# Two layers of linear attention and squared-relu feed-forward: one more pair of tiles by the seven block products in each layer

## The chip, the cores and the metric

The kernel runs on one core of one Trainium2 chip. The metric is the device time of one execution in microseconds (us), the median of several runs. The engines are named as in the profile: PE multiplies matrices (PEld is its loading of weights), ACT applies functions and copies, DVE and POOL do elementwise arithmetic, SP issues most DMA transfers. Each engine carries out its own instructions in the order in which the program names them, and waits where an operand is not there yet.

## The reference

There are 2048 tokens of width D = 640. Two layers, with the same weights, each an attention block and a feed-forward block:

```python
x = x + A(layernorm(x))      # attention, 32 heads of 20
x = x + B(layernorm(x))      # feed-forward, hidden width 1728
x = x + A(layernorm(x))
x = x + B(layernorm(x))

A(x): q, k, v = x @ wqkv, by heads; phi(t) = where(t > 0, t + 1, exp(t)) + 1e-6
      kv = sum over tokens of phi(k) v;  z = sum over tokens of phi(k)
      o  = (phi(q) @ kv) / (phi(q) . z + 1e-6);  returns o @ wo
B(x): h = relu(x @ w1 + b1)**2;  returns h @ w2 + b2
```

All of it is float32. The result is the last x.

## The kernel before

**Tiles and groups.** The tokens are 16 tiles of 128, in 4 groups of 4 tiles (`NT`, `TG`, `NG`). A float32 product is made as three passes of a reduced form: each operand is split into a high part (a rounded copy) and a low part (the rest), and PE adds high x low, low x high and high x high (`mm3`, whose matmuls have line 508).

**Attention, folded.** Since kv is one small matrix for each head, kv and wo are multiplied into one matrix M of 640 x 640 before the feed-forward part of a layer. The attention output of a tile is then phi(q), divided by its denominator, times M. M lies in five row blocks of 128, `M[0]` to `M[4]`, each with its high and low part.

**Feed-forward.** For each group there is FC1 (x @ w1) in 14 chunks c = 0 to 13 of the hidden width (`fc1`, L1234, 15 matmuls of 128x512 for each, 10 for the last), each followed on ACT by relu and square (`act`, L1245 and L1246), and FC2 (h @ w2) in 28 steps (`fc2_step`, L1317). FC2 is made by a scheme that forms a 2 x 2 block product from seven block products instead of eight. Its operands are formed on ACT (`u_hi`, L1289), DVE (`u_lo`, L1298; `s_op`, L1263).

**The attention output inside FC1.** During FC1 of group g the attention output of the next group's four tiles is made. There are two ways:

- `single(g, i)`: one tile. 30 matmuls (L508) at PE after chunk `OUTS[i]` = 4, 7, 10 or 13, into PSUM banks 6 and 7; its operand is the whole tile, split high and low at once (`p_split`, L1345 on ACT, L1347 on DVE).
- `pair(g, j)`: two tiles together, by seven block products of M's 2 x 2 blocks (each 256 x 320) and one piece for the last 128 rows of M ("rest"): 54 matmuls (L1528). They stand at four chunks, `c0 + 4` to `c0 + 7`, where `c0` is `PAIR_AT[j]`, 1 or 6: products 1, 5 and a rest piece `d` at the first, 6 and 2 at the second, 7 and 3 at the third, 4 at the last. The operands are seven blocks of 128 x 256 (`hi`, L1474 on ACT; `lo`, L1478 on DVE), of which four are sums made first on DVE (`s_op` inside `pair`, L1471), and two rest pieces (`rest_hi`, `rest_lo`, L1492). The results are added to x on DVE (L1539).

Ahead of either way each tile is prepared. phi(q) is loaded (`b_load_pq`, SP), its denominator made on DVE (`b_den`: a product L744 and a sum L747), it is divided and turned in 32 x 32 blocks on DVE (`b_blocks`: L753, L754, L756, L465), and ACT moves the blocks to their places (`blocks_move`, L474: four instructions of 32 x 160 for each of four block rows). x is loaded (`b_load_x`). After the output: norm statistics on DVE and POOL (L397, L399, L401, L402), the norm (L407) and its store to DRAM (L435), and the addition of b2 on POOL (`f_bias`, L1214). Then the normed tile is loaded again, turned and split for the next FC1 (`x_in`).

**M's block sums.** A pair needs four blocks (m4, m5, m6, m7) that are sums or differences of blocks of M. `mix_M(g)` makes them in the FC1 of group `MIX_G[layer]`, 1 in layer 0 and 0 in layer 1: `whole` (DVE, L1598), `mix` (POOL, L1609), `high` (ACT, L1618), `low` (DVE, L1622), and `store` (SP, L1626 to L1628), which keeps them in DRAM. `place` (SP, L1631) loads the kept m5 into the upper halves of `M[0]` and `M[1]`. Before, it stands in FC2 behind that FC1, at steps 4 and 8. The others are loaded as units when a pair needs them.

**What sets the order.** Nothing is planned by costs. Every piece of side work is put in a list of events by hand: `at(g, n, f)` puts `f` behind chunk n, or (n >= 14) behind FC2 step n − 14; `on` does the same for a tile's work, where a negative chunk falls into FC2 of the group before, or, for group 0, at chunk 0. Behind each chunk the loop issues in this order: the chunk's matmuls, the next unit's load, relu and square, the products that stand at this chunk, and then the chunk's events in the order in which they were entered: `mix_M` first, then FC2's operands (`ffn_events`), then singles, then pairs. Before, a group with g > `MIX_G` has two pairs, others (but the last group) have four singles.

**Weights.** The units of w1, of w2's seven block products and of m4, m6, m7 are loaded on SP into a ring of six buffers (`RING`, `load_ring`, L371) in the order of their use, which `uses_of` lists. A load is issued once a buffer was used. In group 0, `load_stay` (L381) also loads seven resident FC2 units, one behind each of the chunks 3 to 9.

Of the kernel before, what the change touches and what calls it, by code (L numbers as in the profile page):

```python
# [19 lines left out]
NF = 14  # L20
FL = F - 13 * P
TG = 4
# [4 lines left out]
NG = NT // TG  # L27
# [33 lines left out]
MIX_G = (1, 0)  # L61
# [11 lines left out]
def kernel(  # L73
# [141 lines left out]
    def uses_of(layer):  # L215
        uses = []
        for g in range(NG):
            for c in range(NF):
                uses.append((g, "w1", c))
                if MIX_G[layer] < g < NG - 1:  # L220
                    for j, c0 in enumerate(PAIR_AT):
                        if c0 + 5 <= c <= c0 + 7:
                            uses.append((g, ("m6", "m7", "m4")[c - c0 - 5], j))
            uses += [(g, m, k) for m in ORDER for k in range(1, PAIRS)]
        return uses

# [241 lines left out]
    def blocks_move(yz, js):  # L468
        if len(yz) == 1:
            yz.append(ftile("z"))  # L470
        yv, zv = (a.rearrange("p (c j q) -> p c j q", c=DC, q=B32) for a in yz)
        for j in js:
            for i in range(P // B32):
                nc.scalar.activation(  # L474
                    zv[j * B32 : (j + 1) * B32, :, i, :], yv[i * B32 : (i + 1) * B32, :, j, :], AF.Copy
                )
# [90 lines left out]
    for layer in range(N_LAYERS):  # L567
# [156 lines left out]
        def b_load_pq(t):  # L724
            if t < NT:
                pq[t] = ftile("pqt")
                nc.sync.dma_start(pq[t], pqd[t])
# [9 lines left out]
        def b_load_x(t):  # L737
            xr[t] = x1_at(t)
            nc.sync.dma_start(xr[t], src[t])
# [28 lines left out]
        def b_den(t):  # L768
            b_step(t, 2)

        def b_blocks(t):
            b_step(t, 3)
# [69 lines left out]
        for t in range(NT):  # L842
# [54 lines left out]
            g = list(range(DC)) if t > 0 else []  # L897
# [463 lines left out]
        def at(g, n, f):  # L1361
            events.setdefault((g, n), []).append(f)
# [59 lines left out]
        def after(g):  # L1422
            def on(n, f):
                if n < 0 and g > 0:
                    at(g - 1, NF + N_STEPS + 2 * n, f)
                elif n >= NF:
                    at(g, NF + int(2 * (n - NF)), f)
                else:
                    at(g, max(n, 0), f)

            return on
# [134 lines left out]

        def pairs(g):
            on = after(g)
            both = [pair(g, j) for j in range(2)]
            for p in both:  # L1570
                next(p)
            for i, moves in enumerate(MOVES_AT):
                t = TG * (g + 1) + i
                on(PQ_AT[i], lambda t=t: b_load_pq(t))
                on(DEN_AT[i], lambda t=t: b_den(t))
                on(TURN_AT[i], lambda t=t: b_blocks(t))
                for n, q in moves:
                    on(n, lambda t=t, q=q: blocks_move(yzp[t], (q,)))
                on(PAIR_AT[i // 2] + 1, lambda t=t: b_load_x(t))
                x_in(g, i)  # L1580
            for p in both:
                next(p, None)

        def mix_M(g):
            first = (g * N_STEPS + 2) % SLOTS * 4 * HT + 2 * HT
            v = arena.rearrange("p s j k n -> p (s j k n)")[:, first : first + 4 * D]
            h = [R[:, i, 1].rearrange("p c n -> p (c n)")[:, HT + D * j : HT + D * (j + 1)] for i in range(2) for j in range(2)]
            a, b, q = (h[0], h[3]), (h[1], h[0]), (h[2], h[1])
            if g == 0:
                x1 = x1_odd["tile"]  # L1590
                b, q = (h[1], x1[:, 2]), (h[2], x1[:, 3])
            oq = v[:, : 2 * D].rearrange("p (j m n) -> p j m n", j=2, m=2)
            o6, o4 = (v[:, D * i : D * (i + 1)].rearrange("p (j n) -> p j n", j=2) for i in (2, 3))
            lo, hi = slice(0, HD), slice(HD, D)

            def whole(p):
                for out, m in ((a[p], p), (b[p], 2 + p)):
                    nc.vector.tensor_tensor(  # L1598
                        out=out, in0=M[m][:, 0].bitcast(F32), in1=M[m][:, 1].bitcast(F32), op=ALU.add
                    )  # L1600

            def mix(p):
                for out, x, y, op in (
                    (q[p][:, lo], a[p][:, hi], a[p][:, lo], ALU.subtract),
                    (q[p][:, hi], b[p][:, hi], a[p][:, hi], ALU.subtract),
                    (a[p][:, hi], q[p][:, hi], a[p][:, lo], ALU.add),
                    (b[p][:, lo], b[p][:, lo], a[p][:, hi], ALU.subtract),
                ):
                    nc.gpsimd.tensor_tensor(out=out, in0=x, in1=y, op=op)  # L1609

            def parts(p):
                return (
                    (oq, q[p].rearrange("p (m n) -> p m n", m=2)), (o6, a[p][:, hi]), (o4, b[p][:, lo]),
                )

            def high(p):
                for u, x in parts(p):
                    nc.scalar.activation(u[:, 0], x, AF.Copy)  # L1618

            def low(p):  # L1620
                for u, x in parts(p):
                    nc.vector.tensor_tensor(out=u[:, 1], in0=x, in1=u[:, 0].bitcast(F32), op=ALU.subtract)  # L1622

            def store(p):
                for i, m in enumerate(("m5", "m7")):
                    nc.sync.dma_start(kept[m, 0][:, :, p], oq[:, :, i].bitcast(F32))  # L1626
                nc.sync.dma_start(kept["m6", 0][:, :, p], o6.bitcast(F32))
                nc.sync.dma_start(kept["m4", 0][:, :, p], o4.bitcast(F32))  # L1628

            def place(p):  # L1630
                nc.sync.dma_start(M[p][:, :, HD:].bitcast(F32), kept["m5", 0][:, :, p])  # L1631

            for c, f, p in (
                (0, whole, 0), (0, mix, 0), (2, high, 0), (3, low, 0), (3, store, 0), (3, whole, 1),
                (3, mix, 1), (5, high, 1), (6, low, 1), (6, store, 1),
            ) if g else (
                (1, whole, 0), (1, mix, 0), (2, whole, 1), (2, mix, 1), (3, high, 0), (4, low, 0), (4, store, 0),
                (5, high, 1), (6, low, 1), (6, store, 1),
            ):
                at(g, c, lambda f=f, p=p: f(p))  # L1640
            for p in range(2):
                at(g, NF + 4 + 4 * p, lambda p=p: place(p))

        def ffn_events(g):
            for k in range(PAIRS):
# [69 lines left out]
        for g in range(NG):  # L1715
            ffn_events(g)
        for g in range(NG - 1):
            if g > MIX_G[layer]:
                pairs(g)
                continue  # L1720
            for i in range(TG):
                single(g, i)
        side_last()
        if layer == 0:
            prep_last()
# [1 line left out]
        for g in range(NG):  # L1727
# [9 lines left out]
            last = N_STEPS - PAIRS  # L1737
# [46 lines left out]
```

## Time and profile before

| | us |
|---|---|
| median of 3 runs | 1313.88 (1313.72 to 1313.97) |
| the profiled execution | 1314.4 |
| its span | 1312.7 |
| PE busy | 1305.7 (99%) |
| DVE busy | 920.8 (70%) |
| ACT busy | 745.9 (57%) |
| POOL busy | 237.4 (18%) |
| layer 0, FC1 of group 1 (the edited one), start to end | 361.97 to 426.12 |
| layer 1, FC1 of group 0 (the edited one), start to end | 904.55 to 968.70 |

Matmuls are busy time of PE, weight loads that of PEld, and the two overlap. A row of a timeline has the start in us, the length in us, the engine, the line of the kernel, the operation, its output and inputs by the program's names with their shapes, and a count where several are taken together. Brackets at the end give the idle time of the engine just ahead of it and what ended that. The granted clock of PE is 1.00 of full speed over the whole run.

### The profile page before, as it was taken

How to read it: one execution, taken by the hardware profiler on the slowest of the kernel's cores; microseconds unless marked ns; L12 is line 12 of the kernel's file. 1: busy time of each engine (PE TensorE's matmuls, PEld its weight loads, DVE VectorE, ACT ScalarE, POOL GpSimd, SP SyncE). 2: the span in 40 equal slices, each digit the busy share in tenths (PEclk: the TensorE clock that was granted, in tenths of full speed). 3: DMA queues.
4: the chain of work that ended last, by engine and by line, in shares of the span. 5: the costliest groups of instructions: out<-in, count | busy, mean ns of one | idle time of the engine just before them, and what ended most of it. 6: DMA issues, size and time to landing. Idle time of an engine off the chain costs nothing.

```text
span 1312.7 us, 21122 instructions
## 1 busy us (share of the span) xinstructions
PE 1305.7 (99%) x7441; PEld 1188.5 (91%) x7441; DVE 920.8 (70%) x1685; ACT 745.9 (57%) x1648; POOL 237.4 (18%) x305
## 2 busy tenths in 40 slices
PE   9999999999999999999999999999999999999998
PEld 8888888989988988998988889989899899889888
DVE  7888957757965976843856677677779479579145
ACT  5888967785486476334423232387755834944242
POOL 2334310054032102101012222002330030021000
PEclk9999999999999999999999999999999999999999
DMA  6898985699996996998954456544889779879756
GB/s 195 246 277 268 307 244 168 253 349 386 324 329 213 286 366 229 286 369 297 348 179 126 126 136 173 148 166 176 322 282 373 270 253 324 302 252 314 287 188 220
DMA packets 143071, 339.94 MB, mean 259 GB/s; under 512 B 17318, under 2 KB 67622, under 8 KB 142326
## 3 DMA queue, kind: packets, MB, share of 16 engines
q1 hardware_dynamic: 135734, 316.31, 70.2%
q0 software_dynamic: 7232, 22.29, 6.6%
q8 instruction: 59, 0.97, 0.3%
q14 instruction: 46, 0.38, 0.1%
HBM read 255.92 MB, written 70.78 MB: 249 GB/s over the span
## 4 chain that ended last, share of the span: by engine, by line
PE 93%; DVE 2%; ACT 2%; DMA 1%; issue 0%; SPq 0%; POOL 0%; ACTq 0%; DVEq 0%; POOLq 0%
PE PS L508 30%; PE PS L1234 28%; PE PS L1317 26%; PE PS L1528 4%; PE PS L535 3%; ACT z L494 1%; PE PS L1069 1%; PE PS L1082 1%; DMA st<-in_B_w_dram 1%; PE PS L865 0%; PE PS L656 0%; DMA kept<-uprep 0%; DVE xT L524 0%; DVE uprep L331 0%; DVE r L618 0%
## 5 line engine op out<-in xcount | busy, mean ns | idle before, releaser
L1234 PE MATMUL PS<-xTb,u 128*128 128x512 f32 x1640 | 378.9, 390 | 0.0
L1234 PEld LDWEIGHTS PS<-xTb,u 128*128 128x128 f32 x1640 | 306.4, 188 | 61.7
L508 PE MATMUL PS<-kq,xT 128*128 128x320 f32 (+2 forms) x1575 | 284.4, 335 | 1.4 <-DVE xT L524 1.4
L508 PEld LDWEIGHTS PS<-kq,xT 128*128 128x128 f32 x1575 | 250.4, 188 | 29.1 <-DVE xT L524 2.0
L1317 PE MATMUL PS<-u,arena 128*128 128x320 f32 x1644 | 250.6, 310 | 0.0
L1317 PEld LDWEIGHTS PS<-u,arena 128*128 128x128 f32 x1644 | 243.4, 188 | 0.4
L474 ACT ACTIVATE z<-y 32x160 f32<-32x160 f32 x512 | 171.1, 334 | 40.4 <-DVE y L465 34.5
L1298 DVE TENSOR_TENSOR arena<-R,arena 128x512 fp32r<-128x512 f32 (+1 forms) x200 | 135.2, 682 | 83.0 <-ACT arena L1289 82.6
L1289 ACT ACTIVATE arena<-R 128x512 fp32r<-128x512 f32 (+1 forms) x200 | 116.2, 592 | 132.0 <-PE PS L1317 100.3
L1245 ACT ACTIVATE R<-PS,b1sb 128x512 f32<-128x512 f32 x104 | 71.4, 686 | 116.8 <-PE PS L1234 116.1
L508 PE MATMUL PS<-kh,xh 128*128 128x512 f32 x480 | 124.4, 393 | 0.0
L401 POOL TENSOR_SCALAR rs<-mv 128x1 f32<-128x1 f32 x64 | 32.5, 507 | 475.8 <-DVE mv L399 475.1
L1317 PE MATMUL PS<-uw,arena 128*128 128x320 f32 x660 | 106.1, 309 | 0.0
L508 PEld LDWEIGHTS PS<-kh,xh 128*128 128x128 f32 x480 | 87.3, 188 | 15.2 <-DVE xT L524 0.2
L1317 PEld LDWEIGHTS PS<-uw,arena 128*128 128x128 f32 x660 | 99.2, 188 | 0.3 <-DVE x L1331 0.2
L1263 DVE TENSOR_TENSOR R<-R 128x512 f32<-128x512 f32 (+1 forms) x128 | 88.5, 694 | 14.8 <-ACT R L1246 14.8
L494 ACT ACTIVATE z<-y 32x160 f32<-32x160 f32 x272 | 90.9, 334 | 3.3
L610 ACT ACTIVATE r<-PS 128x512 f32<-128x512 f32 (+1 forms) x64 | 27.6, 433 | 96.6 <-PE PS L508 95.5
L617 DVE TENSOR_SCALAR r<-r 128x512 f32<-128x512 f32 (+1 forms) x64 | 21.3, 332 | 69.7 <-ACT r L610 69.6
L1246 ACT ACTIVATE R<-R 128x512 f32<-128x512 f32 x104 | 65.8, 633 | 3.3
L1331 DVE TENSOR_TENSOR x<-PS,x 128x320 f32<-128x320 f32 x112 | 53.0, 484 | 19.2 <-PE PS L1317 18.4
L1539 DVE TENSOR_TENSOR x<-PS,x 128x320 f32<-128x320 f32 x48 | 23.2, 489 | 45.5 <-PE PS L1528 44.9
(155 smaller groups left out, 1548.4 us busy)
## 6 DMA issues: line engine op xcount, KB each, us to landing
u<-kept SPq DMA_DIRECT2D x113, 640.0 KB, 5.7
u<-kept_w SPq DMA_DIRECT2D x104, 640.0 KB, 5.6
u<-kept SPq DMA_DIRECT2D x56, 320.0 KB, 6.4
kept<-uprep SPq DMA_DIRECT2D x49, 320.0 KB, 5.3
z<-xb SPq DMA_DIRECT2D x160, 80.0 KB, 4.9
u<-kept_m SPq DMA_DIRECT2D x18, 640.0 KB, 4.9
pqt<-pq SPq DMA_DIRECT2D x32, 320.0 KB, 6.4
acc<-r POOLq DMA_DIRECT2D x28, 320.0 KB, 5.3
```

The source lines that it names most:

```text
L474: nc.scalar.activation(zv[j * B32 : (j + 1) * B32, :, i, :], yv[i * B32 : (i + 1) * B32, :, j, :], AF.Copy)
L494: nc.scalar.activation(zv[j * B32 : (j + 1) * B32, :, i, :], yv[i * B32 : (i + 1) * B32, j], AF.Copy)
L508: nc.tensor.matmul(ps, a, b, start=first and i == 0, stop=last and i == 2)
L1234: nc.tensor.matmul(ps, a[:, d, :], bb[:, d, :], start=(d, i) == order[0], stop=(d, i) == order[-1],)
L1245: nc.scalar.activation(r, v, AF.Relu, bias=b1sb[:, c : c + 1])
L1246: nc.scalar.activation(r, r, AF.Square)
L1263: nc.vector.tensor_tensor(out=quad(*out, k), in0=quad(*x, k), in1=quad(*y, k), op=op)
L1289: nc.scalar.activation(u[:, 0], v, AF.Copy)
L1298: nc.vector.tensor_tensor(out=u[:, 1], in0=v, in1=u[:, 0].bitcast(F32), op=ALU.subtract)
L1317: nc.tensor.matmul(ps, x, y, start=opens and k == 0 and p == 0 and e == 0, stop=k == PAIRS - 1 and p == b - a - 1 and e == len(seq) - 1, s ...
L1331: nc.vector.tensor_tensor(out=v, in0=ps, in1=v, op=ALU.add)
L1528: nc.tensor.matmul(ps, x, y, start=m in (1, 5, 2, "d") and i == 0 and e == 0, stop=i == len(todo) - 1 and e == 2, skip_group_check=True,)
```

## The change

In the FC1 of group `MIX_G[layer]`, the tiles 0 and 1 of the next group stay singles, and tiles 2 and 3 become a pair (j = 1, products at chunks 10, 11, 12 and 13). So each layer has one pair more and two singles fewer. Since a pair's preparation stands at other chunks than a single's, the steps of tiles 2 and 3 move: their denominators are at chunks 1 and 3 (were 4 and 7), their block turns at 2 and 4 (were 5 and 8), ACT's moves at 3, 4, 5, 5 for tile 2 and 6, 6, 7, 7 for tile 3 (were 5, 5, 6, 6 and 8, 8, 9, 9), the loads of phi(q) in the FC2 before, or at chunk 0 where there is none (were at chunks 2 and 5), the loads of x both at chunk 7 (were 7 and 10), and the norms at chunk 13 and behind it (were 12 and behind 13). `place` moves from FC2 to chunk 7 of that FC1. The ring gets the units m6, m7 and m4 there: m6 just ahead of the last w1 unit and m7 and m4 just behind it.

```diff
@@ uses_of
-                if MIX_G[layer] < g < NG - 1:
+                if MIX_G[layer] <= g < NG - 1:
                     for j, c0 in enumerate(PAIR_AT):
-                        if c0 + 5 <= c <= c0 + 7:
+                        if (g > MIX_G[layer] or j) and c0 + 5 <= c <= c0 + 7:
                             uses.append((g, ("m6", "m7", "m4")[c - c0 - 5], j))
+            if g == MIX_G[layer]:
+                ms = [v for v in uses if v[0] == g and v[1] != "w1"]
+                last = (g, "w1", NF - 1)
+                uses = [v for v in uses if v not in ms + [last]] + ms[:1] + [last] + ms[1:]
             uses += [(g, m, k) for m in ORDER for k in range(1, PAIRS)]
@@ pairs
-            both = [pair(g, j) for j in range(2)]
+            js = range(2) if g > MIX_G[layer] else (1,)
+            both = [pair(g, j) for j in js]
             for p in both:
                 next(p)
             for i, moves in enumerate(MOVES_AT):
+                if i // 2 not in js:
+                    continue
@@ mix_M
             for p in range(2):
-                at(g, NF + 4 + 4 * p, lambda p=p: place(p))
+                at(g, 7, lambda p=p: place(p))
@@ the list of events
         for g in range(NG - 1):
-            if g > MIX_G[layer]:
+            for i in range(TG if g < MIX_G[layer] else 2 if g == MIX_G[layer] else 0):
+                single(g, i)
+            if g >= MIX_G[layer]:
                 pairs(g)
-                continue
-            for i in range(TG):
-                single(g, i)
```

## The prediction

> **What bounds the kernel now.** I read first the page's busy times, then the busy time by stretches, the chain that ended last by pieces inside the two FC1s that the change edits, and last each engine's timeline there.
>
> ```profile
> span 1312.7 us, 21122 instructions
> PE 1305.7 (99%) x7441; PEld 1188.5 (91%) x7441; DVE 920.8 (70%) x1685; ACT 745.9 (57%) x1648; POOL 237.4 (18%) x305
> ```
>
> PE is busy for 1305.7 of 1312.7 us: what takes matmuls away shortens the kernel, and what makes PE wait lengthens it by the whole wait. The next columns are busy time of PE, PEld, DVE, ACT, POOL, then PE clock, DMA share and GB/s. The first row is FC1 of layer 0 with the block sums (its group 1), the second that of layer 1 (group 0), the third an FC1 of layer 1 with two pairs, the fourth six microseconds inside the second:
>
> ```profile
> 361.97:426.12 64.15, 64.15 (x327) 56.08 (x327) 35.75 (x65) 46.71 (x106) 19.05 (x21) 1.00 0.77 271
> 904.55:968.70 64.15, 64.15 (x328) 56.08 (x327) 46.03 (x72) 46.77 (x107) 26.95 (x26) 1.00 0.84 306
> 1010.94:1073.41 62.47, 62.47 (x316) 54.30 (x315) 37.71 (x78) 42.96 (x104) 7.65 (x10) 1.00 0.75 266
> 934.00:940.00 6.00, 6.00 (x38) 5.65 (x37) 4.82 (x8) 3.99 (x12) 1.38 (x2) 1.00 1.03 393
> ```
>
> In all of them PE never waits; ACT is busy for 69 to 73 per cent of the FC1s, and the DMA queues are full in the fourth (share 1.03). That share is an average; what counts is whether ACT is in time where PE takes over its work, so the chain by pieces (start, length, what) and ACT's timeline follow, in layer 1's edited FC1:
>
> ```profile
> 925.98 10.22 PE PS L1234 x45
> 936.20 4.39 PE PS L508 x30
> 940.60 10.22 PE PS L1234 x45
> 950.82 4.39 PE PS L508 x30
> ...
> 1056.37 2.20 PE PS L1528 x15
> 1061.99 2.19 PE PS L1528 x15
> 1067.61 2.19 PE PS L1528 x15
> 1072.10 1.31 PE PS L1528 x9
> ```
>
> ```profile
> 922.15 2.77 ACT L474 ACTIVATE z<-y 32x160 f32<-32x160 f32 x8 [2.89 <-DVE y L465]
> 924.94 0.69 ACT L1245 ACTIVATE R<-PS,b1sb 128x512 f32<-128x512 f32 x1
> 926.20 1.44 ACT L1618 ACTIVATE arena<-R 128x640 fp32r<-128x640 f32 x3
> 931.70 0.72 ACT L1345 ACTIVATE pTs<-z 128x640 fp32r<-128x640 f32 x1
> 939.72 0.69 ACT L1245 ACTIVATE R<-PS,b1sb 128x512 f32<-128x512 f32 x1
> 940.98 0.62 ACT L1289 ACTIVATE arena<-R 128x512 fp32r<-128x512 f32 x1
> ```
>
> ACT is late here already. The x45 from 925.98 are chunks 5, 6 and 7, 10.22 / 3 = 3.41 each, so chunk 6 ended at 936.20 − 3.41 = 932.8; its relu (L1245) runs at 939.72, 6.9 us behind. Before, nobody waits for that: a single needs one split tile per 10 to 14 us.
>
> **The change part by part.** *Matmuls.* Two singles leave, 30 matmuls of 4.39 us each: 8.78. A pair comes, 2.20 + 2.19 + 2.19 + 1.31 = 7.89. Saved 0.89 us per layer, 1.78 in all. The third stretch above agrees: two pairs in place of four singles, 64.15 − 62.47 = 1.68, 0.84 each. It is a gain only as long as PE still never waits.
>
> *When the pair wants its operands.* Products 1, 5 and the rest piece come behind chunk 10, at 950.82 in layer 1, the rest behind chunks 11, 12, 13. A product of six matmuls costs 6/15 of 2.19, 0.88, so product 5 is wanted at 951.7 and the rest piece at 952.6.
>
> *Layer 1, ACT's queue.* Tiles 6 and 7 now have their block turns at chunks 2 and 4, and ACT's moves at 3, 4, 5, 5 and 6, 6, 7, 7, where they were two and three chunks later. Everything below is in the order in which ACT gets it. The start: tile 5's moves began at 922.15 when DVE had turned it; in the new order DVE does the product and sum for tile 6's denominator first:
>
> ```profile
> 921.27 0.84 DVE L465 STREAM_TRANSPOSE y<-pqt 128x640 f32<-128x640 f32 x1
> 943.62 0.81 DVE L744 TENSOR_TENSOR y<-pqt,zbc 128x640 f32<-128x640 f32 x1
> 944.47 0.82 DVE L747 TENSOR_REDUCE den<-y 128x32 f32<-128x640 f32 x1
> 952.23 0.68 DVE L1263 TENSOR_TENSOR R<-R 128x512 f32<-128x512 f32 x1
> 952.83 0.61 DVE L407 TENSOR_SCALAR xn<-x,mv,rs 128x640 f32<-128x640 f32 x1
> ```
>
> that is 0.81 + 0.82, so 922.15 + 1.65 = 923.8. From there ACT has no gap that I can find, because every move's turn is done ahead of it: 12 block-row moves (tiles 5, 6, 7; a row is 4 instructions, 2.77 / 2 = 1.385) 16.6; relu and square of chunks 3 to 8, 926.20 − 924.94 = 1.26 each, 7.6; the block sums' two high halves, 1.47 with the hand-over, 2.9; tile 5's split 0.63; three FC2 splits (L1289) at 0.6, 1.8; and the pair's first two high halves. Those are in the rows of the pairs in later groups:
>
> ```profile
> L1474 ACT ACTIVATE pTs<-z x42: 400/402/420, 480.6 to 1168.7; 128x256 fp32r<-128x256 f32 x42
> L1478 DVE TENSOR_TENSOR pTs<-z,pTs x42: 381/418/3823, 481.1 to 1170.1; 128x256 fp32r<-128x256 f32 x42
> L1492 DVE TENSOR_TENSOR pTs<-z,pTs x12: 283/284/286, 485.0 to 1158.4; 128x128 fp32r<-128x128 f32 x12
> ```
>
> 0.8 for two. Sum 30.3, so product 5's high half is there at 954.1. The FC2 split just before it, done at 953.7, releases DVE for four instructions in order: L1298 0.69, L1263 0.68, the norm of tile 5 0.61, and then product 5's low half 0.42: 956.1. PE wants it at 951.7. Product 1 is in the same queue: four items of ACT (the FC2 split 0.6, relu and square 1.26, two moves 2.77, and its own high half 0.4) nearer its front, its low half behind these two and tile 5's adds on DVE,
>
> ```profile
> 946.91 0.88 DVE L1412 TENSOR_TENSOR x<-PS,x 128x320 f32<-128x320 f32 x2
> 947.71 0.88 DVE L397 BATCH_NORM_STATS2 bn<-x 128x6 f32<-128x320 f32 x2
> ```
>
> some 2.6 us behind 948.8, at 951.8, so PE waits about 1.0 before product 1 and 3.4 before product 5. **Together 4.4 us.**
>
> *Layer 1, the rest piece.* Its low halves (two L1492, 0.28) are next on DVE, after 956.4. Then the biases of tiles 3 and 5 sit together on POOL, since tile 3's was at chunk 10 already and tile 5's waits for tile 5's norm. What that does to a DVE instruction with two inputs:
>
> ```profile
> 940.03 3.11 POOL L1214 TENSOR_TENSOR x<-x,b2bc 128x640 f32<-128x640 f32 x2
> 941.63 2.07 DVE L1298 TENSOR_TENSOR arena<-R,arena 128x512 fp32r<-128x512 f32 x1 [2.71 <-ACT arena L1289]
> 946.30 0.69 DVE L1298 TENSOR_TENSOR arena<-R,arena 128x512 fp32r<-128x512 f32 x1 [1.02 <-ACT arena L1289]
> ```
>
> 2.07 us where the same one takes 0.69 when POOL is idle: it was held until POOL's bias ended. One held instruction costs at least 0 (rest halves first) and at most two of 1.4, 2.8; I take 2.0, nearer the upper end because both biases are released by the norm that stands ahead of the low half. The Trainium skill, "SBUF — State Buffer", section "Who interferes with whom", says that a vector instruction with two SBUF inputs and a GpSimd instruction that reads SBUF exclude each other for the whole instruction; this trace agrees (2.07 against 0.69), and by it the sum below stays, while mere sharing would at most double the two instructions, 0.6 in place of 2.0, and the sum would be 3.5.
>
> *Layer 0.* Same queue, with more slack: ACT had gaps,
>
> ```profile
> 374.85 2.77 ACT L474 ACTIVATE z<-y 32x160 f32<-32x160 f32 x8
> 386.85 0.69 ACT L1245 ACTIVATE R<-PS,b1sb 128x512 f32<-128x512 f32 x1 [3.08 <-PE PS L1234]
> ...
> 408.24 4.40 PE PS L508 x30
> ```
>
> the moves start at 374.85 + 1.65, and 0.8 more because tile 10's load of 320 KB now stands ahead of tile 9's in the queue (0.33 MB at the 393 GB/s of the fourth stretch): 377.3. One block-sum half less lies behind that point (30.3 − 1.5): product 5's high half 406.1, low half 408.2. PE wants it at 408.24 + 0.88 = 409.1. Margin 0.9; the rest piece behind a bias of POOL may miss by some tenths: **0 to 0.4, taken 0.3.**
>
> *The moved load of the block sums into the matrix, and the extra units.* The kept m5 is loaded back at chunk 7 now, where before it was in FC2. In layer 1 the store before it is the last of these:
>
> ```profile
> 939.64 1.03 SPq L1628 DMA_DIRECT2D kept_m<-arena  x1
> DMA to landing us min/median/max: 8.4/8.4/8.4
> ...
> DMA to landing us min/median/max: 6.4/6.9/7.4
> ```
>
> (the second landing row is that of the load back, L1631). SP takes its queue in order: the stores come at about 941 (their high halves leave ACT at 939.4, 14.7 us of the 30.3 before product 5's), then m6's load, which waits for m6's store, then the two loads back. With the tiles' loads now all ahead of chunk 1 the queue is emptier, so I take some 5 us for the store and not 8.4, and 6.4 to 7.4 for the loads back: 952 to 954. That is after 951.7 and before 956.1: covered by the low half, and next in line if ACT turns out earlier. In layer 0, where PE wants them at 409.1, the stores are past well before: ACT's queue had the gap of 3.08 us there, and the same sum ends at 402 to 405. Behind them on SP wait the x tiles, resident units and chunk 13's weights, the x tiles with about 2 us to spare, chunk 13's weights, used after 960, with more than 5; taken 0. The two loads that leave FC2 were hidden by PE: 0. Eight adds for four, and the norms one chunk later, have the following FC2 as cover: 0. More loads of units: 3 of 640 KB in each FC1, 0.77 and 0.84 of DMA share leave room: 0.
>
> *Sum.* −1.78 + 4.4 + 2.0 + 0.3 = +4.9. The profiled run took 1314.4 us, 0.5 over the median of the runs, 1313.88; the change is of one kind on both, so 1313.88 + 4.9 = **1318.8 us**, slower by 0.37 per cent. About 0.2 per cent, 2.6 us, is what a measurement of this kernel can tell from no change.
>
> **The rivals.** *A, nothing waits.* ACT's gaps are wider than I count and the halves come before 951.7: 1313.88 − 1.78 = **1312.1**. For it: the pairs in other groups run without a wait. Against: there no block sums, singles' splits and biases share the chunks, and here it needs 4.4 us less than the 30.3 that I count. This is the rival on the other side. It decides from the point where product 5's low half lands by 951.7.
>
> *B, a smaller wait.* ACT is 1 to 3 us earlier (fewer items behind a late turn) or the biases do not hold the rest piece: waits of 1 to 4 us, 1313 to **1316.4**. If ACT is early, the load of m5, 952 to 954, is what ends last: 0.3 to 2.3 us.
>
> *C, as forecast.* 4.4 and 2.0 stand to within 2 us: 1316.6 to 1320.8.
>
> *D, late loads.* The load of m5 lands after the low half, because the queue is full: a DMA share of 1.03 stood when the 8.4 us landing began. If the store takes these 8.4 us again from 941, and the loads back, issued at 949.5, do so too, they land at 958 to 959, 2 to 3 us after 956.1: up to **1321.8**.
>
> *E, PE's clock.* A gap could make TensorE run slower for a while. The longest gap of PE in the trace is
>
> ```profile
> 172.13 3.05 PE L508 MATMUL PS<-kq,xT 128*128 128x320 f32 x19 [1.18 <-DVE xT L524]
> ```
>
> 1.18 us, and the clock is 1.00 in every stretch shown, so rows give no drop up to there. If after the 3.4 us before product 5 the clock were half for as long as the gap was, 1.7 us of its work would be left over: **1320.5**. The Trainium skill, "TensorE: Matmul & The Clock Gate", section "What's actually happening", gives half rate after at least one idle window of about 3.4 us; no run here shows it yet.
>
> **How the numbers follow.** C 0.54, A 0.14, B 0.22, D 0.05, E 0.05. The predicted time is that of C. The range runs from A's 1312.0 to 1321.0; C's own is 1316.6 to 1320.8. Faster by over 0.2 per cent needs 1311.25, 0.9 us more than A gives: 0.03, out of A's. The rest of A and B lie within 0.2 per cent, up to 1316.5: 0.33. C, D and E: 0.64.
>
> **What would show it.** In the changed profile: PE's waits in layer 1's edited FC1, by name: product 1 and 5 for L1478, the rest piece for L1492, and layer 0's without one; the FC1's length, 64.15 − 0.9 + 6.4 = 69.7, against 63.3 to 63.7 in layer 0; ACT without an idle row from 923.8 to 954; POOL's two L1214 at about 956. If PE waits for uM's load instead, the m5 load was the bound; if nobody waits, ACT's queue was mis-summed.

## The result, and the profile after

| | before | after |
|---|---|---|
| median of the runs, us | 1314.47 (6 runs) | 1319.84 (6 runs) |
| the profiled execution, us | 1314.4 | 1319.76 |
| FC1 with the block sums, layer 0 | 64.15 | 63.31 |
| FC1 with the block sums, layer 1 | 64.15 | 68.72 |

The changed kernel is slower: the ratio is 1.0037, with a 95% interval of 1.0026 to 1.0047. 1318.8 us had been forecast, a ratio of 1.0037 to the median known then.

In the changed kernel's profile line numbers are 4 to 7 higher than before (behind L1420 one more in the kernels A to D below). The head of the page and the first line of the chain that ended last, and behind them that line of the kernel before:

```profile
span 1318.0 us, 21177 instructions
PE 1305.7 (99%) x7429; PEld 1186.3 (90%) x7429; DVE 931.1 (71%) x1715; ACT 749.2 (57%) x1662; POOL 239.1 (18%) x305
PE 89%; ACT 4%; DVE 3%; DMA 2%; issue 1%; SPq 1%; POOL 0%; ACTq 0%; DVEq 0%; POOLq 0%
...
PE 93%; DVE 2%; ACT 2%; DMA 1%; issue 0%; SPq 0%; POOL 0%; ACTq 0%; DVEq 0%; POOLq 0%
```

The share of ACT and DVE in the chain has grown. The stretches of the two edited FC1s show where (length, then busy time of PE, PEld, DVE, ACT, POOL, then the clock, DMA share, GB/s):

```profile
361.49:424.80 63.31, 63.31 (x322) 55.18 (x321) 38.80 (x75) 48.10 (x113) 17.56 (x19) 1.00 0.81 294
905.08:973.80 68.72, 64.38 (x322) 55.18 (x321) 48.98 (x84) 48.39 (x114) 24.54 (x24) 1.00 0.82 302
```

Layer 0 saves 0.84 us and PE waits nowhere in it. In layer 1, 68.72 − (64.15 − 0.84) = 5.4 us are lost: 68.72 − 64.38 = 4.3 as idle time of PE, and 64.38 − 63.31 = 1.1 in PE's rows around it, which count as busy. PE's timeline of the changed kernel names what it waited for (idle time ahead of a row, and what ended it, in brackets):

```profile
664.40 13.68 PE L512 MATMUL PS<-kq,xT 128*128 128x512 f32 x66 [1.40 <-DMA kq<-kept_kq]
...
936.95 0.41 PE L512 MATMUL PS<-uM,pTs 128*128 128x320 f32 x1 [0.22 <-ACT pTs L1349]
939.06 4.52 PE L512 MATMUL PS<-uM,pTs 128*128 128x320 f32 x29 [1.70 <-DVE pTs L1351]
953.64 1.04 PE L1532 MATMUL PS<-uM,pTs 128*128 128x320 f32 x6
955.63 0.41 PE L1532 MATMUL PS<-uM,pTs 128*128 128x320 f32 x1 [0.95 <-ACT pTs L1478]
957.52 1.44 PE L1532 MATMUL PS<-uM,pTs 128*128 128x320 f32 x8 [1.47 <-DVE pTs L1482]
```

Two places of layer 1 stand out: the single product of tile 5 waits for its split, and product 5 of the pair waits for its high and then its low half. The row at 664.40 is at the start of layer 1, where layer 1's projection weights kq are loaded; it is dealt with below. The spans of the two profiled executions differ by 5.3 us, and −0.84 in layer 0's edited FC1, 4.57 in layer 1's and 1.40 at that row make 5.1 of it; the stretches ahead of these places, between them and behind them change by no more than 0.5 us each. The queue behind the waits, on ACT and DVE of the changed kernel, and the two places where POOL's additions of b2 meet DVE:

```profile
925.20 2.78 ACT L478 ACTIVATE z<-y 32x160 f32<-32x160 f32 x8 [5.39 <-DVE y L469]
955.18 0.40 ACT L1478 ACTIVATE pTs<-z 128x256 fp32r<-128x256 f32 x1
```

```profile
936.93 2.07 DVE L1351 TENSOR_TENSOR pTs<-z,pTs 128x640 fp32r<-128x640 f32 x1 [1.07 <-ACT pTs L1349]
957.04 0.42 DVE L1482 TENSOR_TENSOR pTs<-z,pTs 128x256 fp32r<-128x256 f32 x1
957.71 0.49 DVE L1496 TENSOR_TENSOR pTs<-z,pTs 128x128 fp32r<-128x128 f32 x2
```

```profile
936.79 1.54 POOL L1218 TENSOR_TENSOR x<-x,b2bc 128x640 f32<-128x640 f32 x1
957.49 0.64 POOL L439 DMA_DIRECT2D xb<-xn  x1 [3.61 <-DVE pTs L1482]
958.16 5.14 POOL L1218 TENSOR_TENSOR x<-x,b2bc 128x640 f32<-128x640 f32 x2
```

ACT starts tile 5's moves at 925.20, 20.1 us behind FC1's start, and ends product 5's high half at 955.58, 30.4 us later, without an idle row between. DVE ends the low half at 957.46 and PE goes on at 957.52. The split of tile 5 (L1351) started while POOL's first addition ran and took 2.07 us in place of 0.77. The rest halves (L1496) came before POOL's next two additions, ahead of which POOL first issued the store of tile 5's norm (L439), and were not held; there it was POOL that took 5.14 us for two in place of 3.1.

### The profile page after: what moved, and what is told of

It is laid out like the page before. It is cut to its first block, busy times and chain, and to the rows that moved or that the text cites. A ratio compares the mean times of both kernels' runs of the same rounds, so it can differ in the third digit from the quotient of the medians.

```text
span 1318.0 us, 21177 instructions
## 1 busy us (share of the span) xinstructions
PE 1305.7 (99%) x7429; PEld 1186.3 (90%) x7429; DVE 931.1 (71%) x1715; ACT 749.2 (57%) x1662; POOL 239.1 (18%) x305
## 4 chain that ended last, share of the span: by engine, by line
PE 89%; ACT 4%; DVE 3%; DMA 2%; issue 1%; SPq 1%; POOL 0%; ACTq 0%; DVEq 0%; POOLq 0%
PE PS L512 27%; PE PS L1238 26%; PE PS L1321 25%; PE PS L1532 5%; PE PS L539 3%; ACT z L478 1%; PE PS L1073 1%; PE PS L1086 1%; DMA kq<-kept_kq 1%; ACT z L498 1%; DMA st<-in_B_w_dram 1%; DMA pqt<-pq 0%; PE PS L869 0%; PE PS L660 0%; DVE uprep L335 0%
## 5 line engine op out<-in xcount | busy, mean ns | idle before, releaser
L1543 DVE TENSOR_TENSOR x<-PS,x 128x320 f32<-128x320 f32 x64 | 30.9, 489 | 56.4 <-PE PS L1532 55.6
L1335 DVE TENSOR_TENSOR x<-PS,x 128x320 f32<-128x320 f32 x112 | 53.2, 486 | 18.6 <-PE PS L1321 17.9
```

What stands on the lines that cost most here:

```text
L1335: nc.vector.tensor_tensor(out=v, in0=ps, in1=v, op=ALU.add)
```

## The experiments

The theory: in layer 1 ACT's queue, begun late behind DVE and without a gap, sets when product 5's operand is there; layer 0 has slack. The rivals: a cost that the extra units and loads spread over the kernel (the sum of the stretches above leaves it next to nothing); POOL's hold of DVE; the load of m5. The table has, for each kernel, the length of layer 1's edited FC1, the time from its start to the start of the next FC1, both from its one profiled execution, and the ratio of its runs to those of the kernel before with the 95% interval. "c" marks profiles in which PE's clock fell in that stretch, which costs 1.7 us of PE's work (below).

| kernel | FC1 | FC1 + FC2 | ratio to before |
|---|---|---|---|
| before | 64.15 | 106.39 | |
| changed | 68.72 | 111.13 | 1.0037 (1.0026 to 1.0047) |
| pair in layer 0 alone | 64.15 | 106.76 | 0.9997 (0.9988 to 1.0006) |
| pair in layer 1 alone | 68.62 c | 111.03 | 1.0038 (1.0024 to 1.0051) |
| splits later | 70.5 c | 113.46 | 1.0040 (1.0026 to 1.0054) |
| additions of b2 into FC2 | 70.2 c | 117.78 | 1.0075 (1.0063 to 1.0088) |
| denominator later | 68.63 c | 111.01 | 1.0033 (1.0021 to 1.0046) |
| splits later, additions spread | 65.8 | 112.63 | 1.0042 (1.0030 to 1.0055) |
| these two, and denominator later | 67.6 c | 113.78 | 1.0049 (1.0036 to 1.0062) |
| these three, and m5 by POOL | 64.8 | 111.02 | 1.0037 (1.0023 to 1.0051) |
| A: splits and denominator later, additions early | 67.9 c | 110.87 | 1.0032 (1.0019 to 1.0044) |
| B: A, m5 first, units from chunk 7 | 64.26 | 108.77 | 1.0018 (1.0009 to 1.0027) |
| C: A, m5 first | 65.69 | 108.69 | 1.0011 (1.0002 to 1.0020) |
| D: A, m5 first, units from chunk 5 | 64.26 | 109.39 | 1.0017 (1.0008 to 1.0026) |

### One layer at a time

The conditions on `MIX_G` in the change were made to hold in one layer alone:

```diff
-                if MIX_G[layer] <= g < NG - 1:
+                if MIX_G[layer] + (layer == 1) <= g < NG - 1:
```

for layer 0 alone, with `layer == 0` for layer 1 alone, and so at the other places of the change. Expected:

> The changed kernel with the extra pair in layer 0 alone; layer 1 is as before. Theory (ACT's queue in layer 1 is late, layer 0 has slack): FC1 of group 1 in layer 0 takes 63.3 us, 0.84 less than before, PE waits nowhere in it, and the whole kernel is 0.8 us faster than before, within 0.2 per cent. Rival (the extra units and the moved loads cost something elsewhere, such as the 1.4 us that PE waited for kq at the start of layer 1): 0.5 to 1 us slower than before.

> The changed kernel with the extra pair in layer 1 alone; layer 0 is as before. Theory: all of the loss is here: FC1 of group 0 in layer 1 takes 68.7 us (64.15 - 0.84 + 5.4 of waits), the kernel is 4.6 us slower than before. Rival (a part of the loss comes from layer 0's edit, by way of kq): about 3 us slower.

Layer 0 alone: the stretch of its edited FC1, and PE's wait for kq from the table of waits (us in all, times, longest):

```profile
362.06:425.37 63.31, 63.31 (x322) 55.17 (x321) 38.77 (x75) 47.88 (x113) 17.55 (x19) 1.00 0.83 294
```

```profile
PE PS L512 <- DMA kq<-kept_kq: 0.4, 1, 0.4
```

The 0.84 us are saved, with no wait; over the whole kernel they can't be told from no change, and the rival's 0.5 us slower can't be excluded by the time alone (the interval ends at 0.8 us). Layer 1 alone costs as much as the whole change. So the loss is layer 1's. As for kq: the twelve profiled kernels with the pair in layer 0 run the same instructions up to there, and their waits for kq are 1.40, 0.38, 0.56, 1.19 and 1.29 us in five and none in seven; it differs from execution to execution, and nothing in layer 1's edits decides it. Whether the pair in layer 0 makes it likelier stays open: the two profiles without that pair (before, and layer 1 alone) show none.

Layer 1 alone showed something else. PE's timeline at tile 5's product, and the clock (eighth column) around it:

```profile
937.69 6.06 PE L512 MATMUL PS<-uM,pTs 128*128 128x320 f32 x29 [1.72 <-DVE pTs L1351]
956.08 1.44 PE L1532 MATMUL PS<-uM,pTs 128*128 128x320 f32 x8 [1.08 <-DVE pTs L1482]
```

```profile
936.00:938.00 2.00, 0.31 (x2) 0.31 (x3) 1.64 (x1) 1.92 (x5) 0.96 (x1) 0.99 1.03 396
938.00:940.00 2.00, 2.00 (x9) 2.00 (x8) 1.06 (x2) 1.96 (x5) 0.00 (x0) 0.50 1.02 422
940.00:942.00 2.00, 2.00 (x11) 2.00 (x11) 1.09 (x3) 1.94 (x6) 0.49 (x1) 0.65 1.05 420
```

29 matmuls took 6.06 us, where the changed kernel's took 4.52. The clock fell to half after a wait of 1.9 us, and 2 x 0.50 + 2 x 0.35 = 1.7 us of work were lost by it. Here that cost nothing more: product 5 was late anyway, and its wait shrank from 2.4 to 1.1 us. The Trainium skill, "TensorE: Matmul & The Clock Gate", section "What's actually happening", gives half rate after at least one idle window of about 3.4 us and calls the window free-running; the half rate agrees with this row, the drop after only 1.9 us of idle time does not agree with a full idle window.

### What stands ahead of product 5

FC2's splits in this FC1 later:

```diff
             for k in range(PAIRS):
-                at(g, 6 + k, lambda k=k: u_hi(g, k))
-                at(g, 7 + k, lambda k=k: u_lo(g, k))
+                n = (9, 9, 10, 11)[k] if layer == 1 and g == 0 else 6 + k
+                at(g, n, lambda k=k: u_hi(g, k))
+                at(g, n + 1, lambda k=k: u_lo(g, k))
```

(and the sums behind them at 11, 12, 13, the fifth split at 12).

> The changed kernel with FC2's first splits and sums in layer 1's group 0 three chunks later (ACT's splits at 9, 9, 10, 11 and 12, were 6 to 9 and 11). ACT has three splits of 0.6 us less ahead of product 5's high half, and DVE one split and one sum (0.69 + 0.68) less between it and the low half. Theory (ACT's queue): low half some 3 us earlier, at 954.5; the wait of 3.1 us before product 5 falls to 0.5, that of 2.3 us before tile 5's product stays; FC1 66.0 us; the kernel 2.6 us faster than the changed one. Rival (the load of m5 into the matrix, issued at 947.6 and 948.5 and landed 6.8 us later, ends next): 955.4 in place of 954.5, 1 us of the wait stays and is named for the DMA; the kernel 1.7 us faster than the changed one.

It did not get faster, which neither the theory nor the rival had. The rows of ACT, DVE, POOL and PE at product 5:

```profile
951.70 0.40 ACT L1478 ACTIVATE pTs<-z 128x256 fp32r<-128x256 f32 x1
```

```profile
952.13 3.63 DVE L1482 TENSOR_TENSOR pTs<-z,pTs 128x256 fp32r<-128x256 f32 x1 [0.74 <-ACT pTs L1478]
```

```profile
952.43 3.04 POOL L1218 TENSOR_TENSOR x<-x,b2bc 128x640 f32<-128x640 f32 x2
```

```profile
955.81 1.96 PE L1532 MATMUL PS<-uM,pTs 128*128 128x320 f32 x8 [2.36 <-DVE pTs L1482]
```

The high half came 48.9 us behind FC1's start (903.24), 1.6 us earlier than in the changed kernel (955.58 − 905.08 = 50.5); three splits of 0.6 had been expected. But the low half now fell on POOL's two additions and was held for 3.2 us, so it ended where it had ended before. After the wait the clock fell to 0.62 and 0.52 for 2 us each, 1.7 us more. A hold by POOL is what the prediction had put on the rest piece; here it hit product 5's low half.

The additions of b2 of tiles 1 to 3 were then taken out of FC1, all to FC2's start:

```diff
-            at(0, 4 + 2 * t, lambda t=t: f_bias(t))
+            at(0, NF if layer == 1 and t else 4 + 2 * t, lambda t=t: f_bias(t))
```

> The changed kernel with the additions of b2 to tiles 1, 2, 3 on POOL in layer 1's group 0 moved out of FC1 into the start of FC2. Theory (one queue on ACT sets when product 5 can start, and the wait before tile 5's product only takes a part of it ahead): tile 5's low half takes 0.8 us in place of 2.07, PE's wait before tile 5's product falls by 1.3 us, the wait before product 5 grows by the same, FC1 stays at 68.7 within 0.4. Rival (the held instruction of DVE is a loss by itself, and the waits add up): FC1 67.4 us, the kernel 1.3 us faster than the changed one.

The wait before tile 5's product fell from 1.9 to 0.6 us (0.17 and 0.45), as both expected. The pair's waits, which still ended with product 5's halves, grew from 2.4 to 3.4 us (0.48, 1.44 and 1.47), and without the 1.7 us of the clock FC1 is 68.5 us. That is the theory's 68.7 and not the rival's 67.4: ACT's queue sets the end of the pair, and the held split only took a part of the wait ahead. But FC2 paid. POOL, DVE and PE in its first steps:

```profile
978.63 5.33 POOL L1218 TENSOR_TENSOR x<-x,b2bc 128x640 f32<-128x640 f32 x3
```

```profile
984.43 3.75 DVE L1267 TENSOR_TENSOR R<-R 128x512 f32<-128x512 f32 x1
```

```profile
988.57 1.00 PE L1321 MATMUL PS<-u,arena 128*128 128x320 f32 x5 [1.99 <-DVE arena L1302]
```

DVE, which forms FC2's operands, was held there (3.75 us for a sum that takes 0.68 a few rows later), PE waited for it, the clock fell a second time behind that wait (0.67 and 0.50 over 4 us, another 1.7 us), and FC1 and FC2 together are 117.8 us. Neither theory had FC2 in it.

The start of the queue:

```diff
-                on(DEN_AT[i], lambda t=t: b_den(t))
+                on(DEN_AT[i] + (g == 0 and i == 2), lambda t=t: b_den(t))
```

> The changed kernel with the denominator of tile 6 one chunk later in layer 1's group 0 (chunk 2, behind tile 5's turn, in place of chunk 1 ahead of it). Theory (a queue on ACT without a gap, begun late by the 1.65 us of DVE that now stand ahead of tile 5's turn): ACT's moves begin 1.65 us earlier relative to FC1's start, 18.5 us behind it in place of 20.1, and everything behind them too; FC1 67.1 us in place of 68.7 where PE's clock stays whole. Rival (another wait comes next at once, DVE held by POOL, or the load of m5): FC1 stays above 68.

```profile
924.54 2.77 ACT L478 ACTIVATE z<-y 32x160 f32<-32x160 f32 x8 [3.82 <-DVE y L469]
```

```profile
955.14 0.39 PE L1532 MATMUL PS<-uM,pTs 128*128 128x320 f32 x1 [1.66 <-ACT pTs L1491]
956.80 2.11 PE L1532 MATMUL PS<-uM,pTs 128*128 128x320 f32 x8 [1.28 <-DVE pTs L1482]
```

FC1 starts at 906.02 here, so the moves start at 18.5, 1.6 us earlier, as expected. Tile 5's product does not wait at all. Product 5 does, for 2.9 us, and the clock fell behind it, so FC1 is 68.63; without the 1.7 us of the clock it would be 66.9. The profile names for the first of these waits the high half of the rest piece (L1491), which is next behind product 5's on ACT. The term of 1.65 us is shown at ACT; that FC1 would be as much shorter is worked out with the clock's 1.7 us taken off, and was not measured.

### What is late next

With the splits later, the additions spread over FC2 (tiles 1, 2, 3 at its steps 6, 10, 14) and tile 5's at chunk 13:

```diff
-            at(0, 4 + 2 * t, lambda t=t: f_bias(t))
+            at(0, NF + 2 + 4 * t if layer == 1 and t else 4 + 2 * t, lambda t=t: f_bias(t))
-            on(b + 3, lambda: f_bias(t))
+            on(13 if layer == 1 and g == 0 and i == 1 else b + 3, lambda: f_bias(t))
```

> The kernel with FC2's splits three chunks later, and also the additions of b2 of tiles 1, 2, 3 spread over FC2's steps 6, 10, 14 and that of tile 5 at chunk 13 in layer 1's group 0. Theory (with the splits later, product 5's low half was held 3.2 us by POOL's two additions, and nothing else was in its way): low half at some 49.3 us behind FC1's start; the load of m5 lands at 49.3 to 50.1 and is next; wait before tile 5's product 0.6, before product 5 about 2; FC1 66 us, the kernel 1 to 1.5 us slower than before. Rival (ACT's queue alone was the cause and POOL's hold only ran beside it): no change from the kernel with the splits alone, FC1 over 67.5.

Then also the denominator later, and then also the load of m5 by POOL:

> As the kernel before in this list, with tile 6's denominator behind tile 5's turn too. Theory: no wait before tile 5's product; the halves of product 5 are in time, and what PE waits for is the load of m5, which comes behind the stores of the block sums and m6's load on SP's queue: wait 1 us, FC1 64.3 to 64.7, the kernel as fast as before within 0.1 per cent. Rival (ACT or DVE is still last): the wait is named for a low half.

```diff
-                nc.sync.dma_start(M[p][:, :, HD:].bitcast(F32), kept["m5", 0][:, :, p])
+                (nc.gpsimd if layer == 1 else nc.sync).dma_start(M[p][:, :, HD:].bitcast(F32), kept["m5", 0][:, :, p])
```

> As the kernel before in this list, with the load of m5 in layer 1 issued by POOL in place of SP, so that it does not stand behind m6's load. Theory: it lands some 2 us earlier, PE waits nowhere in layer 1's FC1, 63.4 us, and the kernel is 1.5 us faster than before (both pairs' savings of 0.84). Rival (POOL, which waits for the store to land, holds the norms' and biases' work behind it, or the slower issue on POOL gives the time back): FC1 64 us or more.

PE's waits in the three, in this order, each from the kernel's own timeline or table of waits:

```profile
953.00 1.90 PE L1532 MATMUL PS<-uM,pTs 128*128 128x320 f32 x9 [0.61 <-ACT pTs L1478]
```

```profile
952.08 0.68 PE L1532 MATMUL PS<-uM,pTs 128*128 128x320 f32 x3 [1.38 <-DMA uM<-kept_m]
953.51 1.97 PE L1532 MATMUL PS<-uM,pTs 128*128 128x320 f32 x6 [0.76 <-DMA uM<-kept_m]
```

```profile
963.14 1.11 PE L1532 MATMUL PS<-u,pTs 128*128 128x320 f32 x6 [0.34 <-DMA u<-kept_m]
985.36 4.52 PE L1321 MATMUL PS<-u,arena 128*128 128x320 f32 x29 [0.91 <-DVE arena L1302]
```

In the first the hold is gone and product 5 waits 0.6 us for its high half, not for m5; FC1 is 65.8 us, near the 66 expected, though by another sum: the wait before product 5 had been put at about 2 us, and of the 2.5 us above 63.31 only 1.2 are waits, the rest is in PE's rows. But FC2 behind it waits, as its table of waits says:

```profile
PE PS L1321 <- DVE arena L1302: 2.6, 2, 1.7
```

In the second the halves are in time and the load of m5 is last, by name: 2.1 us, where 1 had been expected. In the third that wait is gone as well. Yet none is faster, because FC2 behind them is slower. In the third kernel, FC2's second 12 us, and the same part in the kernel before (third busy time: DVE):

```profile
980.00:992.00 12.00, 10.87 (x69) 9.79 (x68) 12.00 (x20) 5.39 (x10) 5.39 (x4) 1.00 1.05 302
```

```profile
980.70:992.70 12.00, 12.00 (x84) 12.00 (x83) 11.94 (x23) 5.86 (x11) 0.00 (x0) 1.00 1.05 341
```

DVE was busy for 11.94 of 12 us there in the kernel before already. There was no room for holds by POOL (5.39 us of POOL in that stretch, none before), and PE, which never waited there before, now waits for DVE (0.91 us in the row at 985.36). The third kernel's FC2 took 46.2 us in place of 42.24. That FC1 takes 64.8 and not 63.65 (63.31 and the wait of 0.34) in it the named waits do not explain; the theory had 63.4 us, the rival 64 or more.

So the additions were kept in FC1, at places where DVE has room: tiles 1 to 3 at chunks 4, 7 and 7, tile 5's norm and addition at chunk 8 (kernel A, with the splits and the denominator later too), and then, with the same, the load of m5 ahead of m6's on SP and the resident units later (kernel B):

```diff
-            at(0, 4 + 2 * t, lambda t=t: f_bias(t))
+            at(0, (4, 4, 7, 7)[t] if layer == 1 else 4 + 2 * t, lambda t=t: f_bias(t))
-            on(b + 2, lambda: norm_out(t))
-            on(b + 3, lambda: f_bias(t))
+            e = layer == 1 and g == 0 and i == 1
+            on(b + 2 - e, lambda: norm_out(t))
+            on(b + 3 - 2 * e, lambda: f_bias(t))
```

> The changed kernel with FC2's splits three chunks later and tile 6's denominator behind tile 5's turn in layer 1's group 0, and POOL's additions of b2 kept in that FC1 but away from product 5's halves: those of tiles 1 to 3 at chunks 4, 7, 7, tile 5's norm and addition at chunk 8. Theory (the waits are ACT's queue, POOL's hold, then the load of m5; additions moved into FC2 only moved the loss there, since DVE is full there): low half of product 5 at 47 to 48 us behind FC1's start, PE waits for the load of m5 1 to 2 us and for nothing else, FC2 behind it has no wait; FC1 64.3 to 65.3 us, the kernel 0.5 us faster to 2.5 us slower than before, by whether PE's clock falls after the wait. Rival (DVE, already late, is the bound whatever the order): a low half or an operand of FC2 ends last again.

> As the kernel before in this list, with the load of m5 ahead of m6's load on SP and the resident units' loads from chunk 7 on in place of chunk 3, so that the stores and loads of the block sums meet emptier queues. Theory: the load lands 2 to 3 us earlier, by 46 to 47 us behind FC1's start, PE waits nowhere in layer 1's FC1 (63.3 us), and the kernel is 1 to 1.7 us faster than before. Rival (the resident units now come too late or press on FC2's loads): a wait for a unit or for kq in FC2, and no gain.

Kernel A: the low half is there, and PE goes on only 2.2 us later, with the clock already at half:

```profile
952.43 0.42 DVE L1483 TENSOR_TENSOR pTs<-z,pTs 128x256 fp32r<-128x256 f32 x1 [1.26 <-ACT pTs L1479]
```

```profile
955.09 2.75 PE L1533 MATMUL PS<-uM,pTs 128*128 128x320 f32 x9 [2.33 <-ACT arena L1293]
```

```profile
949.82 1.46 SPq L1639 DMA_DIRECT2D uM<-kept_m  x2
```

```profile
956.00:958.00 2.00, 2.00 (x8) 1.97 (x8) 2.00 (x6) 1.97 (x5) 0.00 (x0) 0.50 1.05 420
```

The wait is put down to a split of FC2, which those matmuls do not read. The load of m5, whose first half was issued at 949.8 and landed 5.1 us later, at 954.9, is what fits; its name does not stand in that row. FC1 is 67.9 us, 66.2 without the clock's 1.7, where 64.3 to 65.3 had been expected, and the kernel is slower than expected too; FC2 behind it has no wait, as expected (110.87 − 67.88 = 43.0 us). Kernel B, from its table of waits:

```profile
PE PS L1321 <- DMA u<-kept: 1.3, 3, 0.6
```

The load of m5 was issued at 942.0 and PE waits for nothing at the pair; FC1 is 64.26 us. Now FC2 waits for its units three times, and FC2 takes 44.5 us in place of 42.24: the loads taken out of FC1 press on FC2. That is the rival's outcome; the theory had a kernel faster than before. Two more kernels tell the order on SP (C) from the later units (D: from chunk 5):

> As the kernel that kept the additions of b2 in FC1, with the load of m5 ahead of m6's load on SP, but with the resident units' loads from chunk 3 on, as in the changed kernel. Theory (what the load of m5 waits for is the landing of the block sums' stores, and those meet the resident units' loads): the load lands 1 us earlier than behind m6's, PE waits for it 1 to 1.5 us, FC1 64.5 to 65 us, FC2 without a wait; the kernel 0 to 2 us slower than before. Rival (the order on SP alone did it): no wait, FC1 63.5 us, and the kernel faster than before by 1 us.

> As the kernel with the resident units from chunk 7, with them from chunk 5 on. Theory (the queues are full through this FC1 and the FC2 behind it, so that what is taken out of the one comes back in the other): waits in FC1 and for units in FC2 together 1 to 2 us, the kernel 0 to 1.5 us slower than before. Rival (there is room between the two): no wait in either, 1.5 us faster than before.

Kernel C at product 5, SP's rows of the load of m5 in it, and kernel D in the table of waits:

```profile
954.71 1.74 PE L1533 MATMUL PS<-uM,pTs 128*128 128x320 f32 x9 [1.48 <-DMA uM<-kept_m]
```

```profile
943.50 5.85 SPq L1639 DMA_DIRECT2D uM<-kept_m  x2
```

```profile
PE PS L1321 <- DMA u<-kept: 1.5, 3, 0.6
```

With the units from chunk 3 on (C), the load of m5 still comes 1.5 us late: its two issues take SP from 943.5 to 949.4, the second held at a semaphore until 948.7 (by the program it is the store of that half that has to land; where POOL issues the load, its wait of 4.43 us is named for such a store). With the units from chunk 5 (D), FC2 waits for units as in B. Both waits are as the theory had them, the times not quite: C's FC1 is 65.7 us and not 64.5 to 65, and D is slower than before by 0.17 per cent, 2.2 us, and not by 0 to 1.5. C has the lowest ratio with both pairs, though its interval overlaps with B's and D's, and it is still slower than before, by 0.11 per cent with an interval that starts at 0.02. No kernel tried beats the one before beyond the interval; the pair in layer 0 alone is the only one that is not slower.

## Why the prediction was right, point by point

*The saving.* Forecast 0.89 us for each layer; measured 0.84 in layer 0, where nothing waits.

*Layer 0's wait.* Forecast 0.3 us, within 0 to 0.4; measured none.

*Layer 1's queue.* The sum of ACT's work from tile 5's moves to product 5's high half was 30.3 us; it took 30.4. From there to the low half it was 2.0 and took 1.9. The start was 0.9 us later than forecast (20.1 us behind FC1's start and not 19.25): the phi(q) of tile 5 landed later, 10.3 us behind FC1's start where it had been 9.2. The rows of DVE that it released, before and after:

```profile
913.73 1.35 DVE L744 TENSOR_TENSOR y<-pqt,zbc 128x640 f32<-128x640 f32 x1 [1.85 <-DMA pqt<-pq]
...
915.36 1.22 DVE L748 TENSOR_TENSOR y<-pqt,zbc 128x640 f32<-128x640 f32 x1 [2.94 <-DMA pqt<-pq]
```

In the changed kernel it is one of three loads issued together. With a single load (before, and the pair in layer 0 alone) 4.9 us passed from its issue to that row, in the changed kernel 6.0. The prediction counted such a load in layer 0, 0.8 us, and not here. So the low half came at 52.4 us and not 51.55, and FC1 lost 5.4 us up to it where 4.4 were forecast: the term that was mis-sized is the start.

*Where the wait stands.* The step "PE waits about 1.0 before product 1 and 3.4 before product 5" failed: PE had idled 1.9 us already before tile 5's single product, whose split stands in the same queue and was also held by POOL, and that came off the wait at the pair (2.4 us of idle time there). Product 1 did not wait, since PE came to it that much later. (In the prediction's working of product 1, 948.8 is a slip: the four items that it lists give 949.1. The 4.4 us do not rest on it.) The chain that sets the end was the one forecast; a second consumer on it was overlooked, and the sum did not need it.

*The rest piece.* Forecast 2.0 us of hold; measured 0: DVE was ahead of POOL by 0.45 us. POOL had first issued tile 5's store, for 0.64 us from 957.49, which the prediction left out. The hold existed at two other places, at tile 5's split here, and at product 5's low half in the kernel with the splits later, where it cost 3.2 us.

*The load of m5.* "Covered by the low half, and next in line": shown, by name, in the kernels where the halves came earlier. It landed 6.8 us behind its issue, at 954.4 and 955.3 in the changed kernel, ahead of the low half at 957.46.

*The sum.* Forecast for layer 1's FC1 69.7 us, measured 68.72: 1.0 less by the start and the rest piece together. Layer 0 came out 0.3 lower. Against these stand 1.4 us of waiting for kq in the profiled execution, which no part of the forecast had. That the ratio came out at the forecast 1.0037 is luck in part: the rest piece's 2.0 us were not there, and the later start and kq, which the forecast did not have, made up for them.

*The clock.* The rival that PE's clock would fall after the waits was given one chance in twenty. In the changed kernel's profiled execution it did not fall (1.00 in both stretches). But the mean granted clock of its other five executions is on record as 0.999, which is also what the profiled execution of layer 1 alone shows with one fall; 59 of the 60 executions of the kernel before beside which the variants were timed show 1.000. So the clock probably fell in most executions of the changed kernel, and the chance was put too low; what that cost of the 1319.84 us is not shown (in layer 1 alone it cost nothing more). In six of the variants' profiles it fell, each time for 1.7 us. That this is the price that the prediction named is luck: it took half rate for as long as the gap, 3.4 us, and here gaps of 1.9 to 3.4 us all cost the same 1.7, which is 3.4 us at half rate.

## What to carry to other kernels

An engine that is 70 per cent busy can still be late, and the sum of its instructions from the last idle row to the operand that is wanted, in the order of its queue, gave the time from that row to the operand to within 0.1 us. The landing time itself was 0.85 us off, by the start of the queue, so work out with the same care what releases its first row; and look for every consumer on that queue, not only for the new one. Before work is moved out of a stretch, look whether the stretch that takes it has room on every engine: here DVE was busy for 99 per cent of a part of the next FC2, and the additions moved there took back nearly all of what FC1 gained or more (3.8 of 3.9 us in the kernel with m5 by POOL); the loads moved there took back 2.1 of 4.5 us in B and 2.7 of 4.5 in D. When DVE and POOL work on the same stretch, place POOL's additions by which DVE instruction they will meet.

## What the runs showed of the hardware that was not expected

PE's clock fell to 0.50 after waits as short as 1.9 us (layer 1 alone, 0.17 and 1.72 us with one matmul between), and stayed whole after waits of 1.9 and 2.4 us in the changed kernel and of 1.9 us before tile 5's product in the kernel with the splits later; each of the seven falls in the profiles cost about 1.7 us of work, whatever the wait. The hold between DVE and POOL goes both ways: POOL's two additions took 5.14 us in place of 3.1 while DVE ran its own two-input instructions, and a DVE instruction of 0.42 us took 3.63 behind two of POOL's. A load of 1280 KB for the next layer, issued at the same step of the same instructions, was waited for up to 1.4 us in five profiled executions and not at all in seven.
